# Key-sum reciprocals on VectorE in place of ScalarE, and a new order table, in a four-layer attention kernel

## The chip, the core and the metric

The kernel runs on one core of one Trainium2 chip. The metric is the device time of one execution in microseconds. Engines are named as in the profile: PE is TensorE, PEld its weight loads, DVE is VectorE, ACT is ScalarE, POOL is GpSimd, SP is SyncE, which here issues DMAs only.

## What is computed

A residual stream x (2,048 tokens, 512 wide, bfloat16) goes through four blocks, A, B, A, B, each of the form x = x + block(layernorm(x)). There are 32 heads of width 16. In the kernel one A and one B together are a round, `L` = 0 or 1.

```python
# A: four segments of 512 tokens; causal softmax attention inside a segment, and a memory of the earlier ones
p = softmax(qs @ ks.T * scale + mask)
o = g * (phi(qs) @ M) / (phi(qs) @ z + 1e-6) + (1 - g) * (p @ vs)
M, z = M + phi(ks).T @ vs, z + sum(phi(ks))
# B: linear attention over all tokens
pq, pk = q @ w_phi, k @ w_phi                                        # per head, 16 x 16
phi_k = concat([softmax(pk), softmax(-pk)]); phi_q = concat([softmax(pq), softmax(-pq)])
kv = phi_k.T @ v;  z = sum(phi_k)
o = (phi_q @ kv) / (phi_q @ z + 1e-6)
```

The change concerns the softmax of `phi_k`: each head's 16 exponentials are summed, and their sum's reciprocal is multiplied into v rather than into the exponentials.

## The kernel before, in words

Tokens lie in 16 tiles of 128 on the partitions; four tiles are a segment of A and a chunk `c` of B. Per round the program records, for each segment: LayerNorm (`ln`), projections (`a_proj`), attention in two halves of two tiles (`a_att`; masked scores on TensorE, exponentials on ACT into the tiles PT, PF and PE, which the profile shows as `p`, `pF`, `pE`), the output projection (`out_proj`), and then the key step of B on the same four tiles (`b_keys`). After the fourth segment four query steps of B follow (`b_query`), in the first round each with the LayerNorm and projections of the next round's A. LayerNorm's result goes through a transposing DMA (`tr`, L364) or through TensorE (`tpe`) into a tile of the pool pX, from which the projections read.

The key step takes tiles in pairs, called units here (the last tiles of chunk 3 go one by one). For a unit: TensorE projects 512 key features for both tiles into PSUM (label BK); ACT takes exp of it and of its negative (kexp, two of 1,024 columns); DVE sums each head's 16 values (Zred, L972) into a tile Z of the pool pS, 128 sums per partition; then come the reciprocals, written into column 16 of each tile's `Vt` (pool pT); TensorE projects v (BV); DVE multiplies it by them (Vt, L1007); TensorE forms kv (KV). In the kernel before, the reciprocals of a pair are formed on ACT: one logarithm over the 128 sums in place (zkl, `pS<-pS`), and for each tile an exponential of the negative (zkl, `pT<-pS`, 64 elements). Single tiles use DVE's reciprocal (rZ, L389), in two instructions of 32 elements. Every ACT operation made by the helper `act` has line L351; evacuations of PSUM made by `evac` are L359 on ACT and L360 on DVE; matmuls made by `mm` are L326, those made by `pair` L341.

The order of the work is not that of the recording. A graph of operations with their reads, writes and buffers is recorded first; then `place` reads the string `ORDER`, a compressed table that holds one global order of all operations, the engine of each (evacuations, key masks and some LayerNorm scalings may run on ACT or DVE) and the buffer slot of each tile. Each engine gets its operations in that order, and so does SP's DMA queue. `emit` derives the semaphore waits from the graph, one wait per engine that must have come far enough; an engine works its list strictly in order. PSUM is four slots of 1,024 float32 columns (pD, shown as `D`), which all matmul results share.

At the head, SP's list holds the loads of x and of the weights, and among them the four transposes (`pX<-p`) that bring the normalized second segment (tiles 4 to 7) into the form that its projections read.

Of the kernel before, what the change touches and what calls it, by code (L numbers as in the profile page):

```python
# [16 lines left out]
D = 512  # L17
H = 32
# [279 lines left out]
class Kernel:  # L298
# [147 lines left out]
    def T(self, pool, cls):  # L446
        return Tile(pool, cls)
# [711 lines left out]
VCOP = set()  # L1159
CAP1 = {"KT": 4, "phiQ": 8, "PhK": 4, "E": 8, "xn": 3, "phe": 3, "phiKT": 2}  # L1160
# [13 lines left out]
c-rlH1GHt=vUXwmSZ&+3ZQHhO+qP}nM$$~$HiJge2)fh%+WRDV$-T+D_l@zt@ngKT_gQnzxvFYbeO2>YYmR-ALkdU(bs;q*fqGCM8bCv61dX8yG=*l+99lq2Xa%jI4  # L1174
YY-J&>lKKN9Y8dp$l|{_>chNK|)9h3KBs|NCpU1p)3F}RD+^W4vK*T0s$IgKx~i@1d$L37OF#Wr~xIQJmiI%kPq@h0jK~ap%#>af>03(K_#dSb)XxRhVD=X3PWZ19;
!eO=n1``2#kbuFbYOPdYA^|U;^}prO*dPz#DiA26Dk2$O)<7G2DfBkQTmy_wX(J08ii^+=r)-9iBlBcmXfr0gQzVkQ*k#c*qLRVGMi)51}u-f&w@gmqC9R0Lx($yoM
oI5C_3F7>*-wJB-B5PzXoi8YqlgU=s9$fv^LHz)BblA@Cz~#p%!yyJ07s0b5}*{DP}tEzE>Zm=VHZD0~fJ@CZWTJJ<=k;ByFu0LXz^@F!RTIWa3{!=GU&YRrzqushC
!9%yh51n~!$4XYqAWCM%Eu^8sTT$m4YV^7SBQy@R~!jJF^Oobvi7KcG+EQ;fBK74}VumDQnI+z83nV=-@h9tNLRzOnhi+dp%B6dNC<FOx3z~nd@*I)`9gKKdWPR0Q^
1?R#-U|bJ`De)UzjU#9gOvK*UA4gIjTnyi0W+;tia07gY-{VG@gzIoWl*a=w2-jl;+<*g7^9uwz2!?;aH~11QBfZ6`m<OieaUeq8h&8bm#>J{w4a;IVjEC{@M-0F$@
CuKCz&bbsD`7>PiPf<(*1#$ljKiol*2Q|b1w-&NI0>n-6xK)L2ABYc(^lMuoA4Zj;yXMKU%+<Uj7#tg%%U$L63@a<_%nXMKum-QF@pC&I39u%FdZAB#E;0d6lc>;+=  # L1180
cUS2QI=!I3E||9Gr`daRDyGCK!eh7=%sH@oRjKvv4=g#%WZTmSII&i7T)ORiYWR95d2%nn`nLE@h$sPK<jn2JXdRZibnuIkv!-7|E^i2(-ZvW^Rj7+zv<4XevwjC_j
~>0u)A@s32{o;uKDWs67^?Q&55g6{9FTM2AVzX^5bhs4xOzLMq&ct*`?s+Cckp5N)K&RE5e@NjiX$RDl9$FvY?%co0uuAjP1Q_!)kVhwv~4Q4BtUr*Ive#ZnXpW8-=
{hhu0geSzty8l|VIG>%GB8OlJRd=v#&ry4Y#T2d>@fXyi*wxBdPfhJN~JcgMtiX^AQwlsv=QB#^iQ)wtQqq<a&CR2TCO>L+F)uzVOgw{|UYDn{_5ly1Clo`)sdaOx?
j)JByu|0L5j&vH2V<5+cT9lPK(R{j&3uqB7p&NJsFXAO!NQ>zv-p1s#ly=ZEN<rIbIqjsBbQm1PBuim@3-90xT1hdvGaaEWbQibNQCdY^DVS#S9KMVr`3inUqj(E_P
O)eo#ina`72{BRN<?v~8}*^S6a`u6B7{&Z4rj&paVs65{j`Vn(lI(n$7wg6pa(dbAL2>6hhum;pQY1Og3r({n!zQx9G{}cn2^fzBTP-_C;^?Pew3XnaSkrVmAN>_=A
j&ib8=$pPCckU^`s;em*dfD8pbm@5vQVAT!AZcVt$Upc?5rj@i_^np|3F+SLbSc8In>c72%>>maFnaeu4*i5?A3e{1nG?DK5>2cmk)TUi1ZhNzbqb51^Xdo7QtKUdS
7G5%1^xe1HpZZXU~Xc`8riaa@q+aUssb11T9@g2J4Tlkx?c!bkZSFXknDkuFg@zDc*J887F_JfEBMU~a%GcmX%$AzY8^^D<t`OSu(i;C0-Z5AzYO#VdIgU#8W3g%WT
b&d8fN6W8VYw1pdUBW}ShxeY&{w%ml<aZ_&3pL0r1#hLjbo#MyTNHi9==_*~LJ9L+>Qx;CnDYyf7<W8KLbJ0o8O?fCi-++z$8E2#Hw3RQwJ*v(5xHISFSg?j~&?deK
X*nzBphxtC&hl|S#|^|bKEVw|7v9NTc{}gor?i82b189}&+uLj5c{~acus+$f~Y9=a5<5a(s4HK#(nubf5H8@KM&wE{3Uni9^8|A@mCZfz9uWmi)R!moQM)J#6ZqV-
_W<zn_p0v2p2Eu6@`d6B2;K$#4Q*mVu{!ySOkff;yW5H>WB+Gi2LwucujG|_Y_ZD<hr7sxWvswebHQ8<|}-QuW~g(qJ@y+4Y8;$9&jb`kcDU|DvP(IL=(|QT!U*IUt  # L1190
EXVe4X#`UB1UPMGetblo5~k9W@nC_&rq-Wkpr-1C0`+MQhPX)Do>kVo_T><)7$BYA4!@&LW9ODw2s`D4|FsK2d4`e1jiz8j)UP5XnVKkxKkbX~hTXA~J~-BBMwrGK(
zYBV`rYM0Sxt+~=E|Lv$76#1;6O$BPM~hj_+c@kG&6Jm+utD)bRAd4%XIMv52wEx+P!qPr*|a*AFemw3&+#rIrNbP%~k9+6iR5^p%4$S(?r!s0tFB8rM)Vvv|Bn#g{
lzZfE#$^l}q7$b&?vEnT^lkfQ*H<ts&4?IOo7L&w}{8UU6)5Q!iQ*;z@pr9x&W{GEFwpb$Oh@bdp{=iGcbMcj!E9Qx1V!l`|R)_^+p;#$aiI2QaeB$+DyZD6{iN#{I
SR>Yo4Pui3u~BRmD9(tpVuxrU&xtR@VX<2r5qm^SxkYRh+r&|^SL_$(#ZIwH>=OsXA#qR~7stex;)1v+E{P86vgoKDidM3<ydqAB&&5e`N<0!*#WnGnxFhb0)8d}EE
^de?@}_toZj1ZkmguB9tH<JN@j`qno``S6OYus)7T<~Q#T(H^eiTn-TiIT=lRt=GL<jjy{wO-ix1y7LC!WjB^1b*Zy2!8O*HX$h3S?XLja0I${7H0^D1R1Ceh^xID_
_f3@`ZdUhs*9VK=zO$<ae^C43uM}kz*yvAlXiRFRf(RU%rv;)c`qCj*{bKupBRid@DobXgNXllD%c9MAcnc)m3#--Bg&IC@0A{GF--$?_`7=DBsI?GE&BuQ8JB8E0f
3=GO0`_)5`=hrpzFJkO^fnnOvrj8D&c8R1Za}r}|O$Qa{N=GL}pw6U)gmwfrD6$=Gs`{8?s}ALVovtg^^KDyy8K2CIUyiYz3v$q<!W7M6WvZ`D_>lmUv>FEW?>Bv;8
# [73 lines left out]
```

## Time and profile before

| | before |
|---|---|
| median of 3 runs | 477.54 us (476.16 to 478.46) |
| the profiled execution | 477.2 us, of which the span is 475.5 us |
| mean granted clock of TensorE | 0.996 |
| DVE instructions | 812, busy 418.5 us |
| ACT instructions | 567, busy 424.1 us |
| TensorE matmuls | 11,583, busy 450.5 us |

Busy times are unions: an engine that works on two overlapping instructions counts once. Matmuls are pipelined and their ends are modelled, so a TensorE that is busy 95% is not at 95% of its peak. A wait is put down to the engine that came last by the profile; where a wait has several causes, the one named may have been done long before. In a row of a window table, the columns are the stretch, its length, the busy time (and instructions) of PE, PEld, DVE, ACT and POOL, the granted clock, the DMA share and GB/s. In a row of a group they are line, engine, operation, output and input tile, shape and count, then busy time and mean ns of one, then idle time before them by releaser. In a row of the timeline they are start, length, engine, line, operation, tiles, shape, count, and in brackets the idle time ahead of it.

### The profile page before, as it was taken

To read this page: it belongs to the slowest core of one execution; us is meant where nothing else is said; L and a number is where in the kernel's file an instruction comes from. 1 tells how busy PE (TensorE), PEld (TensorE's weight loads), DVE (VectorE), ACT (ScalarE), POOL (GpSimd) and SP (SyncE) were. 2 spreads that over 40 slices of the span, in tenths; PEclk is the share of its full clock that TensorE was granted. 3 is DMA by queue.
4 is the path that set the end of the run, shared out by engine and by line. 5 is a ranking of instruction groups with operands and counts; after the bars stand their busy time and mean duration, and the time that the engine had idled before them with its cause. 6 is when DMAs were issued, how large, how long until landed. Compare 5 with 4: busy or idle time off the path is not lost.

```text
span 475.5 us, 25072 instructions
## 1 busy us (share of the span) xinstructions
PE 450.5 (95%) x11583; PEld 296.2 (62%) x11583; DVE 418.5 (88%) x812; ACT 424.1 (89%) x567; POOL 54.7 (12%) x139
## 2 busy tenths in 40 slices
PE   9979999999999999999999999999999999999885
PEld 4447665767667676565555666666666667666542
DVE  6969999999699888987999998998897887898994
ACT  3869999999999998579999999999999999786961
POOL 2301112001011101100220041110020020110000
PEclk9989999999999999999999999999999999999999
DMA  9941292352423132100133334343104404100256
GB/s 233 248 84 39 42 127 56 76 66 48 69 51 60 25 42 33 24 1 4 37 80 70 81 47 72 69 71 59 26 5 81 61 4 70 37 12 3 55 81 204
DMA packets 89388, 30.36 MB, mean 64 GB/s; under 512 B 75954, under 2 KB 89282, under 8 KB 89282
## 3 DMA queue, kind: packets, MB, share of 16 engines
q1 hardware_dynamic: 88450, 28.20, 32.0%
q8 instruction: 91, 1.49, 1.3%
q10 hardware_dynamic: 800, 0.52, 0.4%
q14 instruction: 15, 0.12, 0.1%
q0 software_dynamic: 32, 0.02, 0.0%
HBM read 6.31 MB, written 2.10 MB: 18 GB/s over the span
## 4 chain that ended last, share of the span: by engine, by line
PE 64%; ACT 21%; DVE 12%; issue 2%; POOL 1%; DVEq 0%
PE D L341 40%; PE D L326 21%; ACT p L351 10%; ACT pF L351 7%; ACT pE L351 3%; DVE p L1087 2%; PE D L662 2%; DVE p L1084 2%; DVE X L925 1%; DVE p L360 1%; DVE p L1090 1%; DVE pT L1007 1%; DVE pK L360 1%; PE D L378 1%; DVE pV L360 1%
## 5 line engine op out<-in xcount | busy, mean ns | idle before, releaser
L351 ACT ACTIVATE p<-D 128x1024 bf16<-128x1024 f32 (+1 forms) x220 | 217.5, 1018 | 12.8 <-PE D L341 7.8
L351 ACT ACTIVATE pF<-D 128x896 bf16<-128x896 f32 x128 | 115.7, 927 | 5.1 <-PE D L326 4.5
L326 PE MATMUL D<-pK,pQ 64*128 64x256 bf16 (+3 forms) x1536 | 113.7, 243 | 4.3 <-ACT pF L351 1.9
L326 PEld LDWEIGHTS D<-pK,pQ 64*128 64x128 bf16 x1536 | 55.4, 94 | 40.8 <-ACT p L351 5.2
L326 PE MATMUL D<-pV,pF 64*128 64x34 bf16 x1024 | 76.5, 176 | 1.6 <-issue 0.8
L326 PE MATMUL D<-pW,pF 64*128 64x34 bf16 x1024 | 73.9, 176 | 0.0
L326 PEld LDWEIGHTS D<-pV,pF 64*128 64x128 bf16 x1024 | 57.2, 93 | 5.8 <-ACT pF L351 2.1
L588 POOL TENSOR_SCALAR rstd<-mv 128x1 f32<-128x1 f32 x60 | 15.0, 256 | 359.7 <-DVE mv L581 359.5
L326 PEld LDWEIGHTS D<-pW,pF 64*128 64x128 bf16 x1024 | 53.5, 93 | 1.4
L326 PE MATMUL D<-pV,p 64*128 64x34 bf16 x1024 | 53.1, 176 | 0.6 <-issue 0.2
L351 ACT ACTIVATE pE<-D 128x768 bf16<-128x768 f32 x64 | 52.1, 821 | 1.5 <-PE D L326 0.9
L326 PE MATMUL D<-pW,p 64*128 64x34 bf16 x1024 | 51.7, 176 | 0.0
L326 PEld LDWEIGHTS D<-pV,p 64*128 64x128 bf16 x1024 | 47.0, 93 | 3.3 <-issue 0.7
L326 PEld LDWEIGHTS D<-pW,p 64*128 64x128 bf16 x1024 | 45.4, 93 | 1.6
L326 PE MATMUL D<-tri,two 64*128 64x128 bf16 (+1 forms) x384 | 46.2, 234 | 0.2 <-issue 0.2
L326 PE MATMUL D<-pV,pE 64*128 64x34 bf16 x512 | 45.0, 175 | 0.0
L580 DVE BATCH_NORM_STATS2 stats<-X 128x6 f32<-128x512 bf16 x64 | 43.2, 682 | 2.0 <-DMA X<-in_A_x_dram 1.7
L326 PE MATMUL D<-pW,pE 64*128 64x34 bf16 x512 | 43.2, 175 | 0.3 <-issue 0.3
L341 PE MATMUL D<-pX,WA_k 64*128 64x512 bf16 x256 | 37.3, 383 | 2.8 <-ACT pF L351 2.6
L972 DVE TENSOR_REDUCE pS<-p 128x64 f32<-128x1024 bf16 (+1 forms) x36 | 38.5, 1090 | 1.4 <-ACT p L351 1.2
L925 DVE TENSOR_TENSOR X<-X,D 128x1024 bf16<-128x1024 bf16 (+1 forms) x29 | 32.0, 1107 | 8.4 <-PE D L341 8.3
L341 PE MATMUL D<-pX,WA_q 64*128 64x512 bf16 x256 | 37.6, 384 | 0.6 <-DVE pV L360 0.5
(132 smaller groups left out, 992.3 us busy)
## 6 DMA issues: line engine op xcount, KB each, us to landing
pW<-pV SPq DMA_DIRECT2D x16, 136.0 KB, 3.6
out_dram<-X SPq DMA_DIRECT2D x7, 256.0 KB, 4.2
X<-in_A_x_dram SPq DMA_DIRECT2D x3, 512.0 KB, 5.7
pX<-in_B_wqkv_dram SPq DMA_DIRECT2D x3, 512.0 KB, 5.0
p<-p SPq DMA_TRANSPOSE x76, 2.7
pX<-p SPq DMA_TRANSPOSE x54, 3.3
WA_k<-in_A_wk_dram SPq DMA_DIRECT2D x2, 256.0 KB, 6.8
WB_o<-in_B_wo_dram SPq DMA_DIRECT2D x8, 64.0 KB, 3.6
```

Source lines behind the costliest of these rows:

```text
L326: ins = e.matmul(out_ap, lhsT, rhs, start=st, stop=sp, tile_position=(basep(lhsT), basep(out_ap)))
L341: ins = e.matmul(out_ap, lhsT[64 * hf:64 * hf + 64], rhs[64 * hf:64 * hf + 64], start=k == 0 and i == 0, stop=k == 1 and i == len(lists[hf ...
L351: return self.g.op({"act": (dur, lambda e: e.activation(out_ap(), in_ap(), func, scale=scale))}, reads, writes, opens, label=label)
L360: "dve": ((340 if fast else n / 0.96 + 65), lambda e: e.tensor_copy(out_ap(), in_ap()))}
L378: ins = e.transpose(pb()[:, k * 128:(k + 1) * 128], src()[:, k * 128:(k + 1) * 128], self.ident[:])
L580: v(lambda e: e.bn_stats(self.stats[:, t, :], self.X[:, t, :]), 602, [R("X", t)], [R("st", t)], label="bn")
L588: v(lambda e: e.tensor_scalar(rs, self.mv[:, t, 1:2], LN_EPS, None, op0=ALU.add), 170, [R("mv", t)], [R("rstd", t)], eng="pool", label="rstd")
L662: ins = e.matmul(D.t[c0:, r0 * 8:r0 * 8 + n], r[:, c0:], ones(r, n), start=True, stop=True, tile_position=(r0, c0))
L925: self.v(lambda e: e.tensor_tensor(X(), X(), src(), ALU.add), 65 + 512 * n / 0.96, pr + xr, xr, label="res")
L972: fn = lambda e, sgn=sgn, eo=eo, Z=Z, n=n: e.tensor_reduce(Z.t[:, 0:64 * n].rearrange("p (k s h) -> p k s h", k=n, s=2)[:, :, sgn, :], eo( ...
L1084: v(lambda e, Ns=Ns, Tm=Tm, w=w, shape=shape: e.tensor_tensor(shape(Tm.t[:]), shape(Ns.t[:]), w(), ALU.mult), 600, [Ns, AB[0], AB[1]], [Tm ...
L1087: v(lambda e, N=N, Tm=Tm, w=w, shape=shape: e.tensor_tensor(shape(Tm.t[:]), shape(N.t[:]), w(), ALU.mult), 1131, [N, AB[0], AB[1]], [Tm], ...
```

## The change

For chunks 0 and 1 of the key step in both rounds (`ZKD`), the reciprocals of a pair are formed by DVE's reciprocal, one instruction of 64 elements per tile, directly from the sums. That is eight units: 8 logarithms and 16 exponentials fewer on ACT, 16 reciprocals more on DVE. Chunks 2 and 3 stay as they were. The table `ORDER` is replaced as a whole.

```diff
@@ b_keys
                 Zr = [Z[0], Z[1]]
-                if n == 2:
+                zact = n == 2 and (L, c) not in ZKD
+                if zact:
                     self.act(lambda Z=Z: Z.t[:, 0:128], lambda Z=Z: Z.t[:, 0:128], ACT.Ln, 128, Zr, Zr, psum=False, label="zkl")
                 for k, tt in enumerate(u):
                     Vt = Vts[tt] = self.T(self.pT, "Vt")
-                    if n == 2:
+                    if zact:
                         self.act(lambda Vt=Vt: Vt.t[:, :, :, 16, :], ..., ACT.Exp, 64,
                                  Zr, [Vt[("z", 0)], Vt[("z", 1)]], scale=-1.0, psum=False, label="zkl")
                         continue
                     rz = lambda a, b, Vt=Vt, Z=Z, k=k: (...)
                     for a, b in ((0, 1), (1, 2)) if n == 1 else ((0, 2),):
                         v(lambda e, rz=rz, a=a, b=b: self.recip(e, *rz(a, b)), ..., label="rZ")
@@ module level
 VCOP = set()
+ZKD = {(L, c) for L in range(2) for c in range(2)}
 ...
 ORDER = """
-c-rlH1GHt=vUXwmSZ&+3ZQHhO+qP}nM$$~$HiJge2)fh%+WRDV$-T+D_l@zt@ngKT_gQnzxvFYbeO2>YYmR-ALkdU(bs;q*fqGCM8bCv61dX8yG=*l+99lq2Xa%jI4
...
+c-rlH1&|#_vTZ`~Fo~I&nVFfHnVFfHnVFf%k}cU{W(HeewwPtVzIWtZ+iU;zkN7X*?~B(n_jXrxWme|NlV`dkCJoeudQcx4Kto6Z@gV^;g2vDUnnE*Z4lST1w1U>q2
...
 """
```

What the new table does to the lists: the stages come in the same sequence, and most operations keep their place on an engine within a few positions. Besides the 24 and 16 operations above, fifteen operations that may run on ACT or DVE change sides; in number they nearly cancel. On SP the four transposes of the second segment stand directly behind one another, after a load of x (tiles 8 to 11), the second halves of the key and query weights, the value weights and some of the output weights; before, three loads (x tiles 12 to 15 and two raw weight matrices of B) stood between the four. The matmuls that read them, the projection of the second segment, use another PSUM slot than before.

More of the change, by code (lines that the diff above doesn't have):

```diff
@@ L1178 @@
[L1178 to L1185, printed above, removed]
@@ new lines @@
+?Rn^n`TK3r4~yNDsZC4~&Ls@BnVZLwE*{ARc@TFYz0A4nM%RFb?j(SQrm4;3d3*S9lkGgrDFZ<bc;O1}1=kobVdoU@piGxuGvShEy;DM&eQ!jLV=9j=~|h2@2yj7>-
+}UKo|gD!6e84gW(A*hitGKM&NcRfP<hQu7v*34_3e`*a4fND{g^qm<88BR-6twFeiQoZ{R*Wg>cvkt8fN%#EI}8C&Oc00yE(W4uRF!33tLScnjI^9dt*H*>Nb&gB~~
+x4Q7SJunva8dsqv<fW_ii4D(@r%!9cx7xu)wI0c455iE+m5YeIKsW2Q$-~uR#NpLre#|gLx#$r+&jpJ|(0?vh5uor%Y`H&3X;vDz@vtd2-#pJjK`{7#bj47}Sro>4&
+j3(j$?2W@|1N6tzI2rrkI?M=!nZPmQLf8l&FoYMuVkm>_aSCq0PhdZk$Bj4$%i=(+fXtcU00{mTr(zbEh9BrV6c~s#F)o(FT38jUVP&j>GcX>;$C+3iD`F+AgWIq+F
@@ new lines @@
+2EXC7wh2`+>Q%zD+c2noQnbY1^kTP;}7^0f5B&19~)p=2*T$G^dp8s7#x8pD22!1Fa*L;NQJ>5u_3-gr0Mtqf5J@|f}3#(F2&Pu5<)o?&%hKq3#Z^5B)|yF1Iuw4PN
+f;N6Nk`D8cL0D7S6`TI1lIJKKK+8VI;=DgxCasrq<X7n_^;Yi_LHs?#4w}o~F?bT#O@V1+K&jG@V9LdYVPEDFaDvhXMQxHAmn**dF&{IJUqrRvgHAs5IrJGL(_R@Hi
+Bv6HtWmQ3w^JLbQSM(?*KIP-=;Xpa6xD!VZ`k_hBm}DoO*0sTl32a2iN4QBW-W1lQ34T2GetV{D9r2k<aP&}Z-|9>LErk~9~m5>%E-Q6)NwC20+nqf=OgD$*!gOKGS
+wrKQt2n$BWXsz%{_6c6GdJch?H9gU%}lm?qqT5L)gumv@vag-51$8;D)nQ%M}qBhi;CQ)sgOoOQoHKrysktR@0szoiSE;Xc8RG(T=J!(LWXb!EWxpW4rQ)Y}{N#{_J
@@ new lines @@
+q4XF)ZK)l#rxTcozQ9O`fEpCZ$e)9w3m8Zph}dupIFFiw_$tn$MYMpf;e1+1NofluqwBbpZsHPJO512LC8vY1oj#?{s3UEnPPB(M(_UIe%jp)bpw4syFXD8b!Iy9-5
+91hgkPcByiba?43ht!cw2yYt=X98k(hmBB?&248gog77zK2El1Wo4Sbc~8}7rKMJ=r+co-jsmiQCI3l-Kh`tr7!U-JV~c$B?WUZP2u>InFn$fF2{qoJV$XMj=@to1;
+wST+=F6MO6o_cC?*%?X&jGBaeOYrrMWCW!omDC4&elxn!drz6c^&aX*xp}pfXqD0$h+Qa!KCH`?vz%$FW?3AK(El#>IIYC!|D_h#z7VPC`L+5n@4ZUd{cfCncs>T$M
+lNJiLZSb2c8yGdVkt;ZZ!7C-6ib&$D<Q=jD8ykaKWsj>Gx+EbZn!e2&i3HEP6-c`?uDNxXn(bAPVGOLz{~<pEraYx5#*#w&Rtr{U(jia+7Be4Q@PMY=&Z=@MP0rM!%
@@ new lines @@
+9(G^O^i8%>Z<K>)z<MMu9&o%fCZQz>Rf?IMEZpsa~A>XC?T#s9EYpy5K^F2z+$+*7wirR2nZpUBnA-)dD`34;3&p8Ke<eZd+HgO%1l~Qsp%E;O1OS(@FDK%e$+mwrQ
+a&^8+?Kvi#hZTH`KjY)Pmg|axypB8YR_@5#cr$O|PTZ4^aw$<-?BFA;#V+2?WkfNtlZ_}Vii<}ig%V#=hzJ#(xfl25KHP;f@d@tBCpi^Api`WkzNK%dD|h4W945Y_a
+1kVe#rO0B#SnoaLPQA`0pcb^3L$<XC#>klr@05G;M{ZzVv1PeM;at*h%-D`)D*QuZE=>*aXHaQ{LJM=C4u4>ZY)4l7Pq;HXe#dTU2Y&6iZA&wJs}cT`5Iq_D{zm`b5
++qoR1qyj3Gs|diVEU6RTRTSGcjCT;HUJ0UQ#<zO;i{0MRU<!BoGNjBJq~uig@B3UF1uAoo{e#ahY3**5W3=r>{7*cty!YVv$TF6=_6DkwUztB%+f@C(?>kB7;aTI*2
@@ new lines @@
+!PpF4|(+)-o{nM7uBg>P{jkwrY>A>t}rgRgm%7%Cp{XfZ~N72onV{2g}_-NpCZL-Z6AL=n+POcYtg5Bw7s6>UTpkxg_JKXP`FL*x@VMShV>Jmvx-w<stIi9Di#>?In
+?0iw4UDEf)MVua`~p7TgCUW^kj_$x6<OcqnbRPltL@-uEE8_Q{;ttc$=ikJL~?~CbTftVp4h=*dKm?;*CSz@+WES88lVy<|{uX&Yt!>h$+@s{U_rDB;_E>?(@VvSfQ
+-t$p$Ol%QN<XW*_eBk-wxHu^`h)rUn_(W_M`^5oqN^BEb#SXDk>=wJk8L>y~6MMyH;#1L7o)vA>Inh?#5zS<Cd0u=W4vNF#khm*Oh>PO1xFC**OX9NlTwD>?#SQVLy
+eY1U+v2LYCEBTb;!Dw9JrduDZ^hT*JMq2vLHsCw5|2eI`9{1IU&)s8xo9n0$ouk%cp=)zr{aNZD<4Xfk0i;jWjpyyycDm*JMmh)7vIPhO34qRz3d=6%1)A{mYwDI@>
+}_x94vp3E!7A)M0SxsN+W-gBjwLR$X|q&kEN8Yl#{PzS2<J;lcVGlIa-2@A)m^a@{Me*0%R;1TL#N#GDJR?y=5O6NA{I*WuOd_!{r#+QFT@wR43I<O4UWhlig*g43l
@@ new lines @@
+H!2RTkE^|OpG6UcCxP^OTHWMbJ*rj)5<YMDg#kV$1486nfkWHM5|kmF@KnOsK6^wOz*DubM?GRl{-zv`+2R9=}$PEpxqPdQJ%l1t?;QY%nzrBU-`R+&v^mRaNixlrb
+mi)00vPga!uWiL5E=9jVbKp96@lHF8n9ajgccXF8wQr%S!IY{<U%jF7LS*Fuf<Rg_{f30q)0uq%~@8x1yRR*i-vYK2Xd#aUkf}AcV%2l$LnjvqhuhcbFP~KP9)nG;H
+mg=pBs6OhpViixv*OTN-IZGCjvt?0PM9z_u<rF#96Q9CzwVW%<$}~EyE+<1&DqUWt)}vLZ8l$GkzN&;QCWoppHC2sO->Q4+8}&easqU!!`mTDYlIZW%cdCF+s&~qwI
+)UCLe^BGp0QIAqrUt6ra+oTntLucihF&9M=$N{=Tq_IfOR|X0rZ3CvI;C1C!_{7SMQ)TE<ajk*4OfFyBE4BA*5~B}l}TTaDReSDQDxS9<W`wWUX+v67P($-k{NVLok
@@ L1233 @@
+7|V>|zFPZBNCp&yVQ91luopojc{yVUeSDe<Wdl(V<bQuemR>|6++&8fL!|eL={2}7O<!aA>W#i_h+Tlc<9)=7CYoU|C^&$^S^1^I$3~VM=C6$Bjzm;|rZA6rfxbTQE
+eS>+Q$rxSZ#=-X2=~w+(qX>feLdi__m_;L-%rs}w9rP+cxDVT%4>Yb%4;+~^U(tZJ(R=zn&)L55)kTHMnp@GFEQz{(s<kZ`_`9_3W)SrDEvL(YaR6WD)_Vw{Q80-)Y
+rQ7Q5n%E0lpRr@==zg|D7A6OJg|L7n+ZPQ67;ZJgP~bM*7@Y&p=TK``gunmW+297V6`=FJWQ5w1Pf9u7pI8&rWzI#wU590=;^uV2`Pm0v&kz>Y)Qcnlae;6fDeh;Kd
+thy&XB+lb--dUfooH^_syGHD4GWhrOsULNbJS{uHCfcOT-~E1%a=-v0ju6!e)A
 """
```

80 lines of the change are left out of this document (30 added, 50 removed).

## The prediction, made before the changed kernel had run

> **What bounds the kernel now.** I first read the page's busy line and its chain. TensorE is busy most, but three engines stand near full, and the chain changes engine hundreds of times, so no single figure of the page settles it.
>
> ```profile
> PE 450.5 (95%) x11583; PEld 296.2 (62%) x11583; DVE 418.5 (88%) x812; ACT 424.1 (89%) x567; POOL 54.7 (12%) x139
> PE 64%; ACT 21%; DVE 12%; issue 2%; POOL 1%; DVEq 0%
> ```
>
> So I cut the span by stage: the head, the attention of layer A in each round (40 to 180 and 220 to 400, into which the key work of layer B is woven), and the query stretches between and after. Columns are span, then busy time of TensorE, its weight loads, DVE, ACT and POOL.
>
> ```profile
> 40.00:180.00 140.00, 135.14 (x3986) 94.89 (x3982) 126.24 (x225) 138.18 (x178) 16.38 (x40) 1.00 0.36 60
> 180.00:220.00 40.00, 39.13 (x878) 24.40 (x876) 34.21 (x64) 30.10 (x45) 3.14 (x8) 1.00 0.11 18
> 300.00:400.00 100.00, 97.04 (x2918) 67.47 (x2916) 87.31 (x145) 99.22 (x131) 8.67 (x20) 1.00 0.27 47
> 400.00:440.00 40.00, 39.64 (x864) 25.40 (x860) 35.50 (x60) 31.01 (x44) 3.06 (x8) 1.00 0.14 25
> ```
>
> In the attention ACT is the fullest engine: 138.18 of 140 and 99.22 of 100. TensorE is idle 4.86 and 2.96 us there, DVE 13.76 and 12.69 us. In the query stretches (180 to 220, 400 to 440) it is the other way: TensorE is full, ACT has nine to ten us spare in 40. An ACT instruction taken out of the attention is thus worth most of its time; one taken out elsewhere is worth nothing.
>
> The eight units (pairs of token tiles) that the change touches are chunks 0 and 1 of the key step. The first and the last of their logarithms in each round (four to a round):
>
> ```profile
> 90.62 0.30 ACT L351 ACTIVATE pS<-pS 128x128 f32<-128x128 f32 x1
> 160.36 0.30 ACT L351 ACTIVATE pS<-pS 128x128 f32<-128x128 f32 x1
> 321.14 0.30 ACT L351 ACTIVATE pS<-pS 128x128 f32<-128x128 f32 x1
> 388.39 0.35 ACT L351 ACTIVATE pS<-pS 128x128 f32<-128x128 f32 x1
> ```
>
> All of them lie in the stretches that ACT fills.
>
> **What the edit takes off ACT.** Per unit a logarithm over 128 elements and two exponentials over 64 go: 24 instructions.
>
> ```profile
> L351 ACT ACTIVATE pS<-pS 128x128 f32<-128x128 f32 x36 | 11.2, 316 | 4.1 <-DVE pS L972 2.7 <-DVE pS L1062 1.2
> L351 ACT ACTIVATE pT<-pS 128x64 bf16<-128x64 f32 x28 | 6.7, 263 | 0.2
> 90.96 0.40 ACT L351 ACTIVATE pT<-pS 128x64 bf16<-128x64 f32 x2
> 91.42 0.92 ACT L351 ACTIVATE pF<-D 128x896 bf16<-128x896 f32 x1
> 96.51 0.32 ACT L351 ACTIVATE pS<-pS 128x128 f32<-128x128 f32 x1
> 96.71 0.93 ACT L351 ACTIVATE pF<-D 128x896 bf16<-128x896 f32 x1
> 101.38 0.25 ACT L351 ACTIVATE pT<-pS 128x64 bf16<-128x64 f32 x1
> 101.53 0.91 ACT L351 ACTIVATE pF<-D 128x896 bf16<-128x896 f32 x1
> ```
>
> By the groups' means a unit is 0.316 + 2 x 0.263 = 0.84 us, eight units 6.7. But neighbouring instructions overlap, so I go by start to start: the first unit's three in a row hold ACT from 90.62 to 91.42, 0.80; the second's are spread, 0.20 for the logarithm and 0.15 for an exponential, 0.20 + 2 x 0.15 = 0.50. The mean is 0.65, eight units 5.2 us off ACT, 2.6 per round.
>
> **What it puts on DVE.** Two reciprocals over 64 elements per unit, 16 in all; the trace has none of this size. The nearest are over 32, and the fixed part lies between these two short instructions:
>
> ```profile
> L389 DVE RECIPROCAL pT<-pS 128x32 bf16<-128x32 f32 x8 | 2.4, 327 | 0.0
> L545 DVE CAST Rz<-H 128x64 bf16<-128x64 f32 x1 | 0.1, 145 | 0.0
> L522 DVE MEMSET eps<- 128x1 f32 x1 | 0.1, 59 | 0.0
> ```
>
> If the whole 327 ns were fixed, a reciprocal over 64 would cost 0.33; if it all scaled, 0.65. With 145 fixed it is 145 + 2 x 182 = 509 ns; with 59 fixed it is 59 + 2 x 268 = 595. I take 0.51, the cast being the nearer relative (it reads and writes a tile), and 16 x 0.51 = 8.2 us; ends 5.3 and 10.4. The Trainium skill (VectorE: DVE Perf Modes, "First, the fixed hardware budget") says that the reciprocal is an iterative divide with a repeat count of 8; read as eight cycles an element at 0.96 GHz (the Trainium skill, Trainium Kernel Development and Optimization, "NeuronCore Architecture") that is 8.3 ns an element, 0.53 us and the fixed part, by which estimate the sum for 16 would be about 9.5 us. The 327 ns row agrees with it if the fixed part is the memset's 59.
>
> Four us per round fall on a DVE that has these gaps where the first-round units lie:
>
> ```profile
> 80.00:120.00 40.00, 38.75 (x1160) 28.05 (x1158) 37.31 (x65) 38.97 (x51) 4.41 (x10) 1.00 0.37 63
> 120.00:180.00 60.00, 58.10 (x1752) 40.94 (x1752) 50.66 (x83) 59.68 (x81) 5.10 (x12) 1.00 0.29 49
> ```
>
> Chunk 0 brings 4 x 0.51 = 2.0 us into 2.69 us of idle, chunk 1 the same into 9.34. The second is hidden in DVE's own slack. The first nearly fills it: queued behind such a reciprocal stand key masks, LayerNorm and the attention's divisions, for which TensorE waits. I charge 0.3 us per chunk 0, 0.6 in both rounds; nothing to 4.1 (all eight reciprocals of both chunks 0) are its ends.
>
> The new order also changes the engine of some evacuations. Net, two of 1,024 columns go from ACT to DVE and two of 512 the other way; the rest are pairs of one size that cancel.
>
> ```profile
> L359 ACT ACTIVATE pK<-D 128x1024 bf16<-128x1024 f32 x3 | 3.1, 1032 | 0.0
> L360 DVE CAST pK<-D 128x1024 bf16<-128x1024 f32 x11 | 13.4, 1222 | 2.0 <-PE D L341 1.9
> L359 ACT ACTIVATE p<-D 128x512 bf16<-128x512 f32 x8 | 4.8, 601 | 8.5 <-PE D L341 6.6 <-PE D L894 1.9
> L360 DVE CAST p<-D 128x512 bf16<-128x512 f32 x6 | 4.1, 685 | 0.5 <-PE D L894 0.5
> ```
>
> That is 2 x (1.03 - 0.60) = 0.9 off ACT and 2 x (1.22 - 0.69) = 1.1 onto DVE. I cost it at nothing: it is spread over the head, the tails and the transitions, where ACT has room. DVE's idle time there covers it; without that cover 1.1 us would show.
>
> How much of the 5.2 arrives? All of it if ACT alone set the pace, none if TensorE did. TensorE's idle time in the two stretches, 4.86 and 2.96, leaves room for it, but those gaps are not all ACT's to close. I take a little over half, 2.8 us; ends 0 and 5.2.
>
> **What the new order does at the head.** Here a stall of before has a visible cause. TensorE stops at 23.7 us and starts again at 26.39 with the projection of the second segment.
>
> ```profile
> 23.52 0.22 PE L326 MATMUL D<-tri,two 64*128 64x128 bf16 x2
> 26.39 1.04 PE L341 MATMUL D<-pX,WA_k 64*128 64x512 bf16 x8 [2.65 <-ACT pF L351]
> 13.28 1.30 SPq L364 DMA_TRANSPOSE pX<-p  x1
> 17.14 0.59 SPq L457 DMA_DIRECT2D pX<-in_B_wqkv_dram  x1
> 19.01 0.58 SPq L457 DMA_DIRECT2D pX<-in_B_wqkv_dram  x1
> 19.64 1.32 SPq L364 DMA_TRANSPOSE pX<-p  x1
> 18.31 0.40 DVE L597 TENSOR_SCALAR p<-X,mv,rstd 128x512 bf16<-128x512 bf16 x1
> 26.00:28.00 2.00, 1.61 (x18) 0.97 (x20) 0.00 (x0) 0.29 (x1) 0.00 (x0) 0.94 0.60 108
> 28.00:30.00 2.00, 2.00 (x14) 1.08 (x12) 0.77 (x1) 0.97 (x2) 0.00 (x0) 0.50 0.43 100
> 30.00:32.00 2.00, 2.00 (x18) 0.82 (x14) 1.40 (x5) 1.64 (x3) 0.00 (x0) 0.71 0.32 65
> ```
>
> The label names ACT's pF, but by the program this matmul waits for a PSUM slot that another exponential (the second of p, 21.29 + 2.10) had freed by 23.4, and for four transposed tiles. SP issues those four with three large loads between them; the last goes out at 19.64 and is in by 26.39, 6.7 us later. In the changed program the four stand directly behind one another on SP, and the three loads behind them. The scaled tile that feeds the last is DVE's 50th instruction there, 51st before (18.31 + 0.40 = 18.71), so the last transpose goes out near 19 and, even with before's 6.7, lands by 25.7; with the queue clear I expect 22 to 23. What is late next is the PSUM slot, now freed by the exponential of pE that ends before at 23.77 + 0.82 = 24.59:
>
> ```profile
> 12.80 0.60 ACT L359 ACTIVATE p<-D 128x512 bf16<-128x512 f32 x1 [2.44 <-PE D L341]
> 21.29 2.10 ACT L351 ACTIVATE p<-D 128x1024 bf16<-128x1024 f32 x2
> 23.77 0.82 ACT L351 ACTIVATE pE<-D 128x768 bf16<-128x768 f32 x1
> ```
>
> From 12.80 on ACT runs 17 instructions to its end in both programs, the same ones but for a 896-column exponential in place of a 1,024-column one, so 24.6 stands. The projection starts 26.39 - 24.6 = 1.8 us earlier (ends 0 and 1.8).
>
> After the gap the granted clock falls: 0.94, 0.50 and 0.71 in three windows of 2 us cost 2 x (0.06 + 0.50 + 0.29) = 1.7 us of TensorE, while ACT and DVE wait for it. With the gap cut from 2.7 to about 0.9 us I expect most of that drop to stay out, and take 1.2 of the 1.7. The Trainium skill (TensorE: Matmul & The Clock Gate, "What's actually happening") has the clock halve after an idle window of about 3.4 us, so that by it this gap alone would not have done it. The trace shows 2.65 us of idle ahead of the drop, less than that.
>
> The price of the new load order: one more load of four X tiles and small ones go ahead of the second key and query weights and the value weights. Before, those had landed ahead of their use, and the first matmuls follow the warm-up without a gap; I cost it at nothing, up to 0.5 us if they land late.
>
> **The sum.** The profiled execution took 477.2 us, its span 475.5 and 1.7 around it; the median of the runs is 477.54, 0.3 above. Head -1.8 - 1.2 = -3.0; ACT -2.8; DVE +0.6: -5.2, so 472.0, and 472.3 as a median.
>
> **Rivals.**
> *The clock falls anyway.* If the half-clock stretch is set by a window and not by this gap, 1.2 us of the sum is lost: 473.5. For it: the trace shows the drop after the gap once, and order alone ties the two. The Trainium skill's idle window, named above, speaks for this rival. Chance 0.08.
>
> *TensorE swallows the relief.* If its 95% is real, the 24 instructions only turn ACT's work into ACT's waiting, and the head alone stays: 477.5 - 1.8 = 475.7 without the clock, 474.5 with. For it speaks TensorE's 64% of the chain, against it ACT's 0.78 us of idle in 300 to 400. Chance 0.20, mostly within the bound.
>
> *DVE becomes the bound (slower).* The place is chunk 0 of each round. Once DVE is busy over 39 of 40 us in 80 to 120 (before 37.31, plus 2.0 is 39.3), every reciprocal delays divisions and masks behind it. Price: 8 x 0.51 = 4.1 us, and 1.1 for the evacuations that moved, with the head's gain lost to late weights (+0.5) and no relief seen: 477.5 + 5.7 = 483.2; half of it 480.4. For it: the new load is just at this point. Against it: the reciprocal spares a hand-over from DVE to ACT and back. Chance 0.20.
>
> *The edit does not show.* The order table is replaced whole, so stalls appear and vanish elsewhere, and its net may cancel the rest: 477.5, either side by 2. Chance 0.07.
>
> **How the numbers follow.** Forecast 0.45. A measurement of this kernel can tell about 0.5%, 2.4 us: faster is below 475.1, slower above 479.9. Faster: 0.45 + 0.08, and a quarter of TensorE's rival (0.05), less 0.04 for the forecast's slow edge: 0.54. Slower: 0.20, and a small part of the order's: 0.22. The rest is 0.24. The fast end takes head 3.5, all 5.2 of ACT, no charge on DVE and two us for stalls that the order takes away: 477.5 - 10.7 = 466.8; the slow end reaches to half-way between the slower rival's two prices, 481.8. Range 466.8 to 481.8; the forecast's own 466.8 to 475.
>
> **What would show it.** Right: projections of the second segment starting near 24.6 and no half clock at 28 to 30; ACT about 6 us less busy in total and still over 98% in the attention; DVE about 9 us more; the new reciprocals at 0.5 to 0.6 us. Wrong: DVE full in 80 to 120 with TensorE waiting for DVE tiles; ACT idle in the attention grown by what it was spared; a gap at the head as long as before.

## The result and the profile after

The changed kernel took 470.73 us (470.13 to 471.01) against 477.36 us of the kernel before on the same chip: ratio 0.9865, interval 0.9847 to 0.9883, about 6.4 us less. A later measurement, beside the last experiments, gave 0.9869 (0.9834 to 0.9903). The profiled execution took 470.9 us, of which the span is 469.2. The forecast was 472.3 in a range of 466.8 to 481.8.

The page's busy line and its chain, after:

```profile
PE 447.4 (95%) x11583; PEld 296.9 (63%) x11583; DVE 426.1 (91%) x828; ACT 419.8 (89%) x543; POOL 55.9 (12%) x139
PE 62%; ACT 19%; DVE 14%; issue 2%; POOL 1%; DVEq 0%
```

ACT is 4.3 us less busy, DVE 7.6 us more. The table by stage, after (stretch, length, then busy time of TensorE, weight loads, DVE, ACT, POOL, clock, DMA):

```profile
40.00:180.00 140.00, 134.73 (x3950) 94.54 (x3950) 128.60 (x226) 135.82 (x164) 15.47 (x38) 1.00 0.42 65
80.00:120.00 40.00, 39.20 (x1187) 27.17 (x1184) 36.70 (x66) 38.59 (x46) 1.55 (x4) 1.00 0.47 70
300.00:400.00 100.00, 97.05 (x3003) 69.12 (x2999) 88.79 (x151) 97.86 (x117) 8.43 (x20) 1.00 0.29 49
```

In these windows ACT is 97.0 and 97.9% busy, where the forecast had over 98. DVE has more to do but is not full, and in 80 to 120, where I feared it, it is busy 36.70 of 40, less than before. How much ACT was spared can't be read here: the windows are fixed in time while the work has moved ahead by some 5 us, so they hold other instructions than before's. Windows that hold the same work follow below.

The head, after. The timeline of SP and, last row, of TensorE with the first projection of the second segment:

```profile
13.56 6.54 SPq L364 DMA_TRANSPOSE pX<-p  x4
23.05 1.62 SPq L736 DMA_DIRECT2D pW<-pV  x2
24.72 1.20 SPq L457 DMA_DIRECT2D pX<-in_B_wqkv_dram  x2
24.40 1.03 PE L341 MATMUL D<-pX,WA_k 64*128 64x512 bf16 x8
```

The landing of the transposes from the DMA table of 12 to 32 us (last number: median us from issue to landing):

```profile
pX<-p SPq DMA_TRANSPOSE x4, 2.8
```

And the two stretches in which the clock used to be down:

```profile
26.00:28.00 2.00, 2.00 (x26) 1.02 (x24) 2.00 (x7) 2.00 (x3) 0.00 (x0) 1.00 0.86 260
28.00:30.00 2.00, 2.00 (x92) 1.62 (x88) 1.97 (x5) 1.78 (x3) 0.00 (x0) 1.00 0.86 283
```

The projection starts at 24.40, not 26.39, with no gap ahead of it, and TensorE runs through 26 to 30 at full clock. The same table for before gave a median of 4.9 us for the transposes.

How the lead grows is seen from one line that both programs run in the same place: the attention's divisions on DVE (L874). From the timelines, the first division of all, the last one of round 0's attention, the last one of the first half segment in round 1, and the last of round 1; here of before:

```profile
36.99 0.68 DVE L874 TENSOR_TENSOR p<-D,pS 128x512 bf16<-128x512 f32 x1
189.39 0.69 DVE L874 TENSOR_TENSOR p<-D,pS 128x512 bf16<-128x512 f32 x1
278.89 0.69 DVE L874 TENSOR_TENSOR p<-D,pS 128x512 bf16<-128x512 f32 x1
410.13 0.69 DVE L874 TENSOR_TENSOR p<-D,pS 128x512 bf16<-128x512 f32 x1
```

Of after:

```profile
31.57 0.68 DVE L874 TENSOR_TENSOR p<-D,pS 128x512 bf16<-128x512 f32 x1
184.51 0.69 DVE L874 TENSOR_TENSOR p<-D,pS 128x512 bf16<-128x512 f32 x1
272.96 0.69 DVE L874 TENSOR_TENSOR p<-D,pS 128x512 bf16<-128x512 f32 x1
403.90 0.69 DVE L874 TENSOR_TENSOR p<-D,pS 128x512 bf16<-128x512 f32 x1
```

The leads are 5.4, 4.9, 5.9 and 6.2 us, and 6.3 at the end of the span. These are single executions, and that of before has the half clock at 28 to 31 us in it, which not every execution of before has (see the run that fills the gap). So 5 us are there before any of the changed reciprocals has run.

Between the first and the second of these divisions lies the attention of round 0, between the third and the fourth that of round 1. Windows between them hold nearly the same work in both programs, but for the change. Before:

```profile
36.99:189.39 152.40, 147.45 (x4352) 103.12 (x4350) 137.23 (x244) 148.94 (x191) 17.95 (x44) 1.00 0.35 57
278.89:410.13 131.24, 126.53 (x3802) 87.83 (x3798) 113.70 (x201) 128.90 (x166) 14.56 (x34) 1.00 0.31 52
```

After:

```profile
31.57:184.51 152.94, 147.57 (x4370) 103.62 (x4366) 140.92 (x258) 148.34 (x181) 16.94 (x42) 1.00 0.39 60
272.96:403.90 130.94, 126.60 (x3818) 89.18 (x3814) 118.09 (x214) 128.06 (x153) 16.34 (x38) 1.00 0.31 51
```

With half of the changed reciprocals in each, the stretches are as long as before (152.94 against 152.40, 130.94 against 131.24). ACT is busy only 0.6 and 0.8 us less, where 2.6 per round had been worked out, and idle 1.1 and 0.5 us more. This reading gave the first theory: the head is the gain, and the edit that the change is named after brings nothing. It was half right.

### The profile page after: what moved, and what is told of

It reads as the page before. It is cut to its first block, busy times and chain, and to the rows that moved or that the text cites. A ratio compares the mean times of both kernels' runs of the same rounds, so it can differ in the third digit from the quotient of the medians.

```text
span 469.2 us, 25086 instructions
## 1 busy us (share of the span) xinstructions
PE 447.4 (95%) x11583; PEld 296.9 (63%) x11583; DVE 426.1 (91%) x828; ACT 419.8 (89%) x543; POOL 55.9 (12%) x139
## 4 chain that ended last, share of the span: by engine, by line
PE 62%; ACT 19%; DVE 14%; issue 2%; POOL 1%; DVEq 0%
PE D L341 40%; PE D L326 20%; ACT p L351 10%; ACT pF L351 6%; ACT pE L351 3%; DVE X L925 2%; PE D L662 2%; DVE pT L1008 1%; DVE stats L580 1%; DVE p L1088 1%; POOL rstd L590 1%; DVE pQ L647 1%; DVE p L874 1%; PE D L378 1%; DVE p L601 1%
## 5 line engine op out<-in xcount | busy, mean ns | idle before, releaser
L588 POOL TENSOR_SCALAR rstd<-mv 128x1 f32<-128x1 f32 x60 | 17.4, 296 | 353.0 <-DVE mv L581 352.8
```

The source lines that it names most:

```text
L588: v(lambda e: e.tensor_scalar(rs, self.mv[:, t, 1:2], LN_EPS, None, op0=ALU.add), 170, [R("mv", t)], [R("rstd", t)], eng="pool", label="rstd")
```

## The experiments

All ratios are to the kernel before on the same chip, with the interval behind.

**The loads moved behind the transposes, alone.** Before's order, with SP's list changed in one place:

```diff
 SP: transposes of the second segment
-pX<-p, load X, pX<-p, load raw weights, pX<-p, load raw weights, pX<-p, pW<-pV x2
+pX<-p, pX<-p, pX<-p, pX<-p, load X, load raw weights, load raw weights, pW<-pV x2
```

> The kernel before, with one thing of the new order alone: the three loads (x tiles 12 to 15 and two raw weight matrices of B) that stood between the four transposes of the second segment are put behind them on SP. Logarithms stay on ACT. If the head is the cause (theory 1): the projection of the second segment starts at about 24.6 us instead of 26.4, the half clock at 28 to 31 us is gone, and the end is 3 to 5 us earlier, 472.5 to 474.5. If the gain comes from ACT's relief in the attention (theory 2): the head gains under 2 us and most of that is lost again, 476 to 477.5.

Measured 0.9969 (0.9943 to 0.9995), about 1.5 us faster, less than theory 1's 3 to 5 and, by the number alone, within theory 2. In the profiled execution the gap and the half clock were gone, but something else was late. From its SP timeline:

```profile
22.15 1.05 SPq L457 DMA_DIRECT2D pX<-in_B_wqkv_dram  x2
23.93 2.20 SPq L736 DMA_DIRECT2D pW<-pV  x2
```

From its DMA table (KB each, median us to landing):

```profile
pW<-pV SPq DMA_DIRECT2D x2, 136.0 KB, 6.5
```

And its chain (start, us, what):

```profile
23.93 6.70 DMA pW<-pV
30.63 0.46 issue
31.09 0.95 PE D L326 x46
```

The small copy that swaps V (`pW<-pV`), issued right behind the two raw weight loads of 512 KB, took 6.70 us to land, and TensorE waited for it. The half clock was not gone for good either: in 8 of the 12 executions the mean granted clock was 0.995 or 0.996, as one window at half clock leaves it (last section); the profiled one was not among them. The changed kernel has the raw weights behind the copies.

**The same with the changed kernel's order of loads.** The two copies go ahead of the two raw weight loads; nothing else moves:

```diff
-pX<-p x4, load X, load raw weights, load raw weights, pW<-pV x2
+pX<-p x4, load X, pW<-pV x2, load raw weights, load raw weights
```

> The kernel before with the loads on SP in the order that the changed kernel has: four transposes, the load of X, the two copies that swap V, then the two raw weights. Nothing else moves; the exponentials stay on ACT. The earlier run with all three loads ahead of the copies lost 1.7 to 2.1 us on a copy that landed 6.7 us after its issue. Theory 1a (that wait was what kept the loads' move from bringing what the changed kernel has in the head): ratio 0.991 to 0.995, 2.5 to 4.5 us under before, and no TensorE wait on the copy at 30 us. Theory 1b (the compute order in the head is what brings it, not the loads): as the earlier run, ratio 0.996 to 1.0.

Measured 0.9936 (0.9914 to 0.9959), 3.1 us faster. From its DMA table:

```profile
pW<-pV SPq DMA_DIRECT2D x2, 136.0 KB, 3.4
```

And its SP timeline:

```profile
23.41 1.33 SPq L736 DMA_DIRECT2D pW<-pV  x2
24.78 1.71 SPq L457 DMA_DIRECT2D pX<-in_B_wqkv_dram  x2
```

The copy lands in 3.4 us instead of 6.5, and the mean granted clock was 0.998 or more in all ten executions. Theory 1a holds, at the lower half of what it expected: about half of the changed kernel's gain is the place of three loads.

**Is it the gap that lowers the clock?** Before, with eleven unused matmuls put into the 2.65 us gap (in outline):

```diff
+F = self.T(self.pD, "fill")          # a PSUM tile that nothing reads
+for _ in range(11): matmul(F, onesb, onesb)   # 128 x 512, placed ahead of the second segment's projection
```

> The kernel before, with 11 matmuls of 512 columns on constants added ahead of the projection of the second segment, in the gap in which TensorE waits for the transposes; their results are not used. The gap stays as long for the data, but TensorE is busy in it. If the idle gap lowers the clock: no half clock at 28 to 31 us, and 1 to 1.7 us faster, 475.7 to 476.4. If the drop is not tied to the gap: the half clock stays and the time is that of before, 477.4, or a little above.

From its timeline of TensorE:

```profile
24.52 2.55 PE L1149 MATMUL D<-onesb 128*128 128x512 bf16 x11
27.75 0.61 PE L341 MATMUL D<-pX,WA_k 64*128 64x512 bf16 x4 [0.68 <-DMA pX<-p]
```

And its window of 28 to 30:

```profile
28.00:30.00 2.00, 2.00 (x28) 1.26 (x26) 0.07 (x1) 0.92 (x1) 0.00 (x0) 1.00 0.47 110
```

The clock stays at 1.00 where it was 0.50. One profile of each kernel does not show that the gap is the cause, since before often runs through without the fall: of its 88 executions measured beside the experiments, 49 have a mean granted clock of 0.998 or more, and 37 have 0.996 or less, as a window at half clock leaves it. The counts do show it: with the gap filled none of twelve executions has 0.996 or less, of before's on the same chip 15 of 29. The time is 0.9974 (0.9948 to 1.0), 1.2 us less with work added, an interval that reaches to no change. The price of a fall is sharper in before itself: executions at 0.996 or less took 2.3 to 2.5 us longer in the median than those at 0.998 or more, in each of three sets (479.44 against 477.08, 480.21 against 477.74, 480.43 against 478.17). The row of 27.75 also names what the gap waited for, the transposed tile.

**The reciprocals on DVE, alone.** Before's order, each unit's three ACT instructions replaced by two DVE reciprocals in their places:

```diff
+ZKD = {(L, c) for L in range(2) for c in range(2)}
 # ORDER as before, with zkl x3 -> rZ x2 in place
```

> The kernel before with its own order, and the reciprocals of chunks 0 and 1 on DVE, each at the place in the order where its exponential stood; nothing else moves. Theory 1 (the head is all): no change within 1 us, 476.5 to 478.5, since ACT's relief turns into ACT waiting for TensorE. Theory 2 (ACT's relief): 2 to 4 us faster, 473.5 to 475.5. If DVE were the bound in chunk 0: 1 to 5 us slower.

Measured 1.0033 (1.0006 to 1.006), 1.6 us slower. Its windows between the same divisions as above:

```profile
37.19:191.49 154.30, 148.22 (x4352) 102.93 (x4350) 139.78 (x253) 147.99 (x179) 17.97 (x44) 1.00 0.35 56
280.84:413.39 132.55, 126.73 (x3802) 87.98 (x3798) 116.81 (x210) 127.78 (x154) 14.57 (x34) 1.00 0.32 51
```

And one of its waits (engine, tile and line waited for, us in total, times, longest):

```profile
ACT pF L351 <- PE D L326: 7.5, 14, 2.5
```

For the same work, less twelve instructions of ACT in each, ACT is busy 0.95 and 1.12 us less, but the stretches are 1.90 and 1.31 us longer than before's, at full clock, and TensorE with the same matmuls is idle longer too (6.08 us against 4.95, 5.82 against 4.71). ACT waited 4.5 us on this line before. The fullest engine was not the one that set the pace. Part of the 1.6 us may be the clock in the head: it is 0.996 or less in 9 of the 12 executions, against 15 of before's 29.

**Both parts in before's order.** The loads of the run at 0.9936 and the reciprocals on DVE:

> The order of before with the loads on SP as the changed kernel has them and with the reciprocals on DVE; the rest of the order untouched. Theory A (without the new order the reciprocals bring nothing): the product of the two parts measured alone, 0.9936 times 1.0033, ratio 0.994 to 1.0. Theory B (the reciprocals on DVE begin to pay when the head no longer covers it): 0.989 or below.

Measured 0.9942 (0.991 to 0.9974), 2.8 us faster, as the loads alone within the intervals, which is theory A. The two stretches of attention are 153.51 and 133.11 us here and 152.68 and 131.13 with the loads alone, so in the old order the reciprocals again bring nothing. The two parts that can be named do not add up to the changed kernel; the other 3.5 us need the rest of its order.

**New order up to the first key exponential, before's from there on, and the reverse.** The cut is at about 76 us. The first has the reciprocals on ACT, the second on DVE; each mixed table has buffer slots of its own. In outline:

```diff
 new head:  ORDER = after[: first kexp] + before[first kexp :]     # logarithms stay on ACT
 old head:  ORDER = before[: first kexp] + after[first kexp :]     # reciprocals on DVE
```

> The new order up to just before chunk 0's first exponential over the keys of layer B (about 76 us, so the whole head, the projections of the second segment and the first attention's divisions), from there the order of before; the key-sum reciprocals stay logarithm and exponential on ACT throughout, so no DVE reciprocal is in this kernel. Theory 1 (the gain is made in the head, by work that is placed earlier there, and the reciprocals on DVE bring nothing by themselves): about 5 us under before, 473 to 475 us against 479, ratio 0.987 to 0.992; within 2 us of the changed kernel. Theory 2 (the gain needs ACT relieved and the order behind it): ratio 0.996 to 1.0, since the loads' move alone gave 0.997.

> The other half: the order of before up to the same place (about 76 us), then the new order with the key-sum reciprocals on DVE. Theory 1 (all in the head): within 1.5 us of before, ratio 0.997 to 1.003. Theory 2 (relief of ACT and the later order): 3 to 5 us under before, ratio 0.989 to 0.994. Between the two lies what the trace of the changed kernel suggests of the rest: 1 us between the rounds and 0.3 us in round 1, ratio 0.997.

Measured 0.9946 (0.992 to 0.9973), 2.6 us, and 0.9973 (0.9943 to 1.0003), 1.3 us. By theory 1 the first should have had 5 us, which its interval excludes, so theory 1 fell; but theory 2's 0.996 and more is missed as well, and the second fits theory 1 or what lies between the two. The halves make 3.9 us together, not 6.4: part of the gain seems to need both. From the timeline of the new head, the divisions that stood above for both kernels:

```profile
33.07 0.68 DVE L874 TENSOR_TENSOR p<-D,pS 128x512 bf16<-128x512 f32 x1
186.90 0.69 DVE L874 TENSOR_TENSOR p<-D,pS 128x512 bf16<-128x512 f32 x1
408.24 0.69 DVE L874 TENSOR_TENSOR p<-D,pS 128x512 bf16<-128x512 f32 x1
```

It is 3.9 us ahead of before at the first division, 2.5 at the end of round 0 and 1.9 at the end of round 1: in this execution the old order behind it gives back part of the lead, and in the measured time what is left is no more than the loads alone had brought. Nor is the head's own lead the same in each execution: the first division starts at 31.57 to 32.43 us in the five profiles with the whole head of the changed kernel and its order behind, at 33.07 here, and at 33.50 with the loads alone.

**The changed kernel without one of its parts.** First with the logarithms and exponentials back on ACT, at the places where the new order has the reciprocals; then beside the ACT neighbours that they have before; then at the first ACT place that starts after the unit's last reduction had ended in the trace of the changed kernel:

```diff
-ZKD = {(L, c) for L in range(2) for c in range(2)}
+ZKD = set()
 # ORDER as after, with rZ x2 -> zkl x3 on ACT
```

> The changed kernel with its new order, but the reciprocals of chunks 0 and 1 back on ACT as logarithm and exponentials, at the places where DVE's reciprocals stand. Theory 1: as fast as the changed kernel within 1 us, 470 to 471.7. Theory 2: 2 to 4 us slower than it, 472.7 to 474.7. If the new order relies on the spared hand-over, slower by more.

> The changed order with the key-sum reciprocals back on ACT as logarithm and exponential, each put beside the same ACT neighbours as in the kernel before, not where the DVE reciprocal stands. Theory 1 (head is all, the edit brings nothing by itself): within 1.5 us of the changed kernel, ratio to before 0.986 to 0.990. Theory 2 (the new order was made for the spared ACT time and has no room for the exponentials): 3 us or more over the changed kernel, ratio to before 0.993 or above; the eight units times 0.65 us of ACT, 5.2 us, are the most that it should cost without new waits.

> The changed order with the key-sum reciprocals back on ACT, logarithm and both exponentials of a unit at the first place among ACT's work that starts after the unit's last reduction ended in the trace of the changed kernel. The run with the logarithms beside their old neighbours had one wait of 5.1 us of DVE on them, at 325 us, with a TensorE stop and 6.8 us at half clock behind it, which made about 6.7 us; before it that run was 2.4 to 2.6 us behind the changed kernel. Theory A (in the new order ACT's spared time counts: 8 units of 0.65 us): 2 to 5 us over the changed kernel, ratio to before 0.990 to 0.997. Theory B (the edit brings nothing by itself, all is the order): within 1 us of the changed kernel, 0.985 to 0.989.

Measured 1.0174 (1.0136 to 1.0212), 1.0047 (1.0028 to 1.0066) and 1.0005 (0.9979 to 1.0032), that is 8.3 and 2.2 us slower than before, and no change. Against the changed kernel these are 15, 8.5 and 6.5 us (6.0 by the medians of the last, which ran beside it): in this order, the edit is worth a lot. Why shows in the waits, here of the first:

```profile
DVE pT L1007 <- ACT pT L351: 11.2, 5, 5.0
```

The same wait in the last:

```profile
DVE pT L1007 <- ACT pT L351: 5.3, 2, 4.9
```

Its timeline of DVE, then of ACT, around the one long case:

```profile
317.51 1.21 DVE L972 TENSOR_REDUCE pS<-p 128x64 f32<-128x1024 bf16 x1
318.64 0.40 DVE L597 TENSOR_SCALAR p<-X,mv,rstd 128x512 bf16<-128x512 bf16 x1
323.95 2.36 DVE L1007 TENSOR_TENSOR pT<-D,pT 128x1024 bf16<-128x1024 f32 x2 [4.91 <-ACT pT L351]
318.99 1.03 ACT L351 ACTIVATE p<-D 128x1024 bf16<-128x1024 f32 x1
...
322.40 1.03 ACT L351 ACTIVATE p<-D 128x1024 bf16<-128x1024 f32 x1
323.31 0.32 ACT L351 ACTIVATE pS<-pS 128x128 f32<-128x128 f32 x1
```

And the window of the clock's grid in which TensorE stands for it:

```profile
322.66:326.08 3.42, 0.38 (x4) 0.00 (x0) 2.13 (x2) 1.37 (x4) 0.00 (x0) 1.00 0.58 124
```

DVE has the sums at 318.7 and wants their reciprocals at 319.0. The logarithm stands behind five exponentials that ACT still has queued, so DVE waits 4.91 us, TensorE gets nothing and stops for 3.3 us, and the clock is halved behind it. In the changed kernel DVE forms the reciprocal itself and goes on. At the division ahead of this unit the run is 1.7 us behind the changed kernel (316.44 against 314.72), at the next one 6.1 (334.18 against 328.08). So most of the loss is this one hand-over, not the 5.2 us of ACT's time that the eight units were costed at. The logarithm could not stand earlier, since the order is one list over all engines and the reduction itself stands behind those exponentials in it. With the reductions moved up as well the hand-over may cost less; that wasn't tried, so it stays open whether an order made for logarithms on ACT could be as fast.

**The three loads back between the transposes, in the changed kernel.**

> The changed kernel with the three loads back between the four transposes, as before has them. Theory A (the loads are a part of their own, worth the 3 us that they brought in the order of before, ratio 0.9936): 3 us over the changed kernel, ratio to before 0.991 to 0.995. Theory B (all that the changed kernel wins hangs on the head): 5 us or more over it, ratio 0.997 or above.

Measured beside a second run of the changed kernel:

> The changed kernel once more, on the chip and in the rounds of the three runs beside it, so that these can be compared with it and not only with before. Ratio to before 0.985 to 0.988, as the first time.

0.9984 (0.9957 to 1.001) against 0.9869: the loads are worth 5.0 us in the new order by the medians, 5.5 by the ratios, as theory B had it. SP's last transpose in its timeline:

```profile
19.93 2.33 SPq L364 DMA_TRANSPOSE pX<-p  x1
```

TensorE's wait behind it:

```profile
PE D L341 <- issue: 3.5, 1, 3.5
```

And the window after the wait:

```profile
28.74:32.15 3.41, 3.41 (x23) 1.71 (x21) 0.00 (x0) 1.43 (x2) 0.00 (x0) 0.50 0.07 20
```

In before the last transpose went out at 19.64 and took the queue 1.32 us; here it is 19.93 and 2.33. The gap is 3.5 us against 2.65, and the half clock is back, by the mean granted clock in 11 of the 12 executions. That is more than the 3 us that the same move brought in before's order. In the new order, without the loads' place nearly nothing of the gain is left, and without the reciprocals on DVE, in the orders tried, nothing: the parts do not add, they need each other.

## Why the prediction was right, and where it was not

The time and the sign were right, and so was the half of the sum that lies in the head. The other half was right by luck: 2.8 us were expected from ACT's relief, which brought nothing, and about as much (3.5 us) came from the rest of the new order, which had been costed at nothing. The stated range, from 10.7 us faster to 4.3 slower, was wide enough to hold either.

- **Head, -3.0.** Right in mechanism: the projection was forecast at 24.6 and came at 24.40, the half clock stayed out, and the loads alone brought 3.1 us on the chip. The two parts of it were 1.8 and 1.2: before's executions at full clock have a median of 477.74 us beside 475.66 with the loads moved, 2.1 us, and the fall that was spared, 2.3 to 2.5 us in 37 of 88 executions, is about 1 us in the mean. Undersized as a whole: the profile has a lead of 5.4 us at the first division, against 3.5 with the loads alone. The rest must lie in what else is new in the head, its evacuations, masks and other loads, which I had costed at nothing; no run separates these. The new head in front of the old order suggests that the rest is kept only where the later order fits it.
- **Loads that go ahead cost nothing.** Right for the list that the changed kernel has, but by less of a margin than I saw: with the copies of V behind the raw weights, half of the gain was lost. I had weighed only the weights that move ahead, not what stands behind large loads.
- **ACT relief, -2.8.** This step failed. The 24 instructions did go, but with the edit alone they took only 2.0 us of ACT's busy time with them (422.1 against 424.1, in the changed kernel 4.3 with the evacuations), not the 5.2 read from start to start. Nor did these 2 us arrive: between the same divisions the attention stayed as long in the changed kernel and grew by 1.90 and 1.31 us with the edit alone, which came out 1.6 us slower. "TensorE swallows the relief", priced at 474.5, was right on this term; the time came out lower, at 470.7, since the new order gave more. "ACT over 98% in the attention" was wrong: 97.0 and 97.9%.
- **What the edit brings instead** is the hand-over from DVE to ACT and back, which I named only as an argument against the slower rival. In before, DVE's multiplication waited for ACT's part 0.3 us in all (its group, last column); in the new order one logarithm in ACT's queue costs DVE 5 us.
- **DVE, +0.6.** The new row below: 0.536 us, against 0.51 taken, 8.5 us in sum against 8.2. The estimate from the Trainium skill (VectorE: DVE Perf Modes, "First, the fixed hardware budget") of about 0.59 with the fixed part is 10% over it. No long wait for the new reciprocals shows in the changed kernel; in before's order the reciprocals did cost 1.6 us, which the slower rival had the right sign for, at a third of its price. Which wait made these 1.6 us stays open, and part of them may be the clock (above).
- **The clock falls anyway.** Wrong as forecast: in none of the ten executions of the changed kernel is the mean granted clock below 0.998. Its thought of a window was right (below), and the forecast, too, took the fall for something that before always has, which it hasn't.

The multiplication's group in before:

```profile
L1007 DVE TENSOR_TENSOR pT<-D,pT 128x1024 bf16<-128x1024 f32 x28 | 33.1, 1215 | 2.4 <-PE D L341 2.0 <-ACT pT L351 0.3
```

And the new reciprocals' in the changed kernel:

```profile
L389 DVE RECIPROCAL pT<-pS 128x64 bf16<-128x64 f32 x16 | 8.5, 536 | 0.1
```

What stays open: which part of the rest of the new order brings the remaining 3.5 us. The profiles of the changed kernel and of loads and reciprocals in before's order part in the head, in both rounds and between them, at no one place.

## What to carry to other kernels

An engine that is 99% busy in a stage need not set its pace: take its work away in the old order and look whether the time follows before counting on it. A short step that goes from one in-order engine to another and back costs what stands queued ahead of it there, so price it by the queue, not by its own duration, and an edit that removes it may pay only together with an order that uses it. In a DMA queue look at what stands directly behind a large load; a small copy or a transpose that TensorE waits for goes ahead of it.

## What the runs showed of the hardware

**The clock falls by a window's share, on a fixed grid.** In the fourteen profiles at hand the granted clock is either 1.00 or 0.50, and every stretch of full clock between two falls, and every half-clock stretch ahead of the tail, lasts a whole multiple of 3.41 us (before: 23.89 us, seven times 3.41, then 3.41 at half, then 443.73, 130 times). Laid on that grid, the clock fell behind a window in which TensorE was busy for a small part, whether or not the window was ever idle for long. The window ahead of the fall in before:

```profile
24.33:27.74 3.41, 1.35 (x18) 0.85 (x20) 1.49 (x6) 1.09 (x3) 0.00 (x0) 1.00 0.78 140
```

The busiest window with a fall behind it, in the run of the old head:

```profile
88.56:91.98 3.42, 1.96 (x92) 1.71 (x94) 2.44 (x6) 2.54 (x3) 0.00 (x0) 1.00 1.17 196
```

And the emptiest full-clock window without one, before the tail, in the run with all three loads behind the transposes:

```profile
27.43:30.84 3.41, 2.00 (x22) 0.70 (x16) 3.41 (x7) 2.65 (x4) 0.00 (x0) 1.00 0.58 136
```

Busy 1.35 (40%) and 1.96 us (57%) fell, 2.00 us (59%) did not; the eight windows that were at most 41% busy all fell. In the last 15 us of the span three windows at 48, 55 and 56% did not fall, so the bound is rough, as the matmuls' ends are. The Trainium skill (TensorE: Matmul & The Clock Gate, "What's actually happening") has a free-running window of 3413 ns, which the traces confirm, and the fall after an idle one, which they do not: a window that is 43% idle was enough once, and every one that was 59% idle or more. The grid lies elsewhere in each execution (the first window at full clock starts at 3.85 us in before, at 6.95 in the run with all three loads behind the transposes, 3.10 later, which is no multiple of 3.41). So whether a gap of two or three us lowers the clock should depend on where it lies on the grid and on the small gaps beside it: in the old head's window the longest gap was 1.12 us.

**One program falls in some executions and not in others.** A window at half clock takes half of 3.41 us out of some 475, which lowers the mean by 0.0036. In the seven profiles without a fall ahead of the tail the mean granted clock is 0.9977 to 1.0, in the seven with one or two 0.9907 to 0.9962, so the mean tells the two apart in executions that were not profiled. By it the clock fell in 37 of 88 executions of before (two more, at 0.997, can't be told), which fits a grid that lies elsewhere each time; and a single profile does not tell whether a kernel has the fall.

**A small DMA lands later right behind large ones.** In single executions, the 136-KB copy took 3.4 us to land ahead of two 512-KB loads and 6.5 right behind them; in before, issued 3.4 us after the second of them (22.40 against 19.01), it took 3.9.
